# Causal attention and a gated expert: the scale of the gated values from the longest rows of v

## Chip, cores and metric

One core of a Trainium2 chip runs the whole program. The metric is device time in microseconds (us) of one execution; the kernel before took 555.05 us in the median of three runs (553.56 to 556.57).

## What is computed

The reference, cut to what matters. Batch 4, 12 heads, 448 positions, head size 64; weights come as 64-bit floats, the rest as 32-bit ones.

```python
scores = q @ k.T / 8, masked causally
attn = softmax(scores)
x = (attn @ v) laid out as [1792, 768]
a = x @ w1; b = x @ w2          # 768 x 1024 each
out = ((a * b) @ w3) @ w_out    # 1024 x 1024, 1024 x 768
```

## The kernel before, in words

All heavy products run on TensorE, most as sums of three half-precision products: a number is split into a scaled high part and a remainder. So each operand needs a scale (a power of two) that keeps it inside the range of 16-bit floats.

*Weights first.* The 64-bit words are decoded to fp32 on ScalarE (L727, L732), VectorE (L734, L737, L742) and GpSimd (L742). w3 and w_out are multiplied together once, in fp32: blocks of w3 are turned on TensorE (L824), copied out by ScalarE or VectorE (L830, L831) as `w3t`, and multiplied with `wof` (L836, 128 products). The result, and the 16 column blocks of w1 and w2 (`w16_0` to `w16_15`), get a scale from a sum of squares: ScalarE squares (L423), TensorE totals over partitions (L436, one column), VectorE makes the scale (L439, L442, L444); then a high part (`scaled`, L775 to L779) and a remainder (L459, L782) are made. A decoded block lives in one of four `da` tiles until its remainder is made.

*Attention.* The 48 heads go as 24 pairs, six per batch. A pair's scores (L612) are masked and their maxima taken on VectorE (L635), the exponentials on ScalarE (L639), the high part on any of three engines (L665, L667, L669), the remainder on VectorE (L672), both turned by DMA and multiplied with v (L692, L697). The result, x, is written as high and low part (L706, L709). `take_v` loads v for half a batch into `vr`, and ScalarE squares it (L423, sum into `vam`) to scale v; the squares themselves go to a `da` tile and are not used.

*Gating.* For each batch, `gate` multiplies x with w1 and w2 (L960 to L962), the two results are multiplied on VectorE, scaled by `y` and split, and `project` multiplies with the product of w3 and w_out (L1020 to L1022) and sends rows out. `norms` finds `y`: it multiplies x with itself on TensorE (L911, 24 products per batch: the largest squared length of a row of x is on the diagonal), takes the maximum (L914 to L917), combines it with the weights' scales and spreads the largest over partitions in `scales` (L407 to L418, one product with a diagonal, L410).

*Order.* Nothing runs in the order it is written. Each step is put into a list with a due time and a choice of engines, and a planner (`Program.order`) simulates all engines and writes out one instruction order for each. The numbers of `PLAN` set due times; an engine then runs its instructions strictly in that order. At the beginning TensorE has nothing to multiply, so `idle_work` gives it products of a tile of ones (L318), four at a time; the planner puts them wherever nothing else is ready.

```python
due += PLAN["wo1"]
take_wo(g, due + PLAN["wo"][g])
...
for _ in range(PLAN["nwarm"]):
    idle_work()
```

Of the kernel before, what the change touches and what calls it, by code (L numbers as in the profile page):

```python
# [26 lines left out]
PLAN = dict(nc=10, wstep=12.3531, soft=-605.1474, w0=476.7288, w34=1.8539, ab=3.6303, out=1.8146, gap=762.8813, lat=251.8676, begin=528.4141, wlead=403.7739, urgent=-286.1889, flex=536.535, sc=-408.2686, vo=420.0393, av=-116.9027, x=-168.3035, qlead=-2186.9998, rlead=-350.7116, v0=1307.3227, v1=8.0035, gram=2, nf=3, h0=-1, hv=0, ns=7, wo0=95.4929, wo1=14.6091, wom=-114.98, w3a=536.4028, w3l=90.5355, wd=-391.0133, wh=745.1126, wl=-928.1541, fin=-157.1358, ev=466.0051, po=[-164.0323, -537.4847, -467.5965, -398.0017, -379.2563, -815.7532, 309.0872, 47.1817, -120.6631, -601.6638, -125.3147, -350.4396, 41.4761, -121.6103, 339.5862, -519.8836, -967.096, -525.6425, 211.87, -136.3489, 191.5148, 668.7091, 243.9157, -640.695], wo=[-156.3639, 185.1511, 155.7329, -52.0715, 196.0473, -222.9949, 297.9082, 432.3035], w3=[15.1689, 214.9782, -115.2249, -1402.9929, -542.2877, 32.1711, -584.6361, 255.7376], tw=[-80.0272, -1064.4391, -227.6554, 134.6056, 384.2709, -735.5482, -250.8318, -265.1624, 67.0919, 261.8515, -168.3921, -339.4492, -398.6288, -878.4922, -309.2601, -175.1905], slack=0.62, pflex=-492.7855, fq=2, hlead=1597.3824, stick=248.1205, wfrom=6, join=0, quick=6, nwarm=34, w3h=[-97.0267, 4.4249, -687.8448, -92.0666, -119.591, 136.5231, 431.7171, 88.0246])  # L27
# [235 lines left out]
def tile_causal_attention_moe(ctx: ExitStack, tc: tile.TileContext, q, k, v, w1, w2, w3, wo, out):  # L263
# [156 lines left out]

    def squares(dst, src, junk, n, due, reads, writes):
# [64 lines left out]

    def take_v(b, half, due):
# [409 lines left out]
    def norms(b, due):  # L897
# [8 lines left out]
        def products():
            for c in range(4):
                n = min(P, S - c * P)
                for d in range(KD):
                    x = xb[:, d, 0, c * P : c * P + n]  # L910
                    nc.tensor.matmul(ps[:n, c * P : c * P + n], x, x, start=d == 0, stop=d == KD - 1)  # L911

        prog.add(due, (PE, 4 * KD * t_mm(P), products), [("xt", b % 2, d) for d in range(KD)], [key])
        prog.add(due, (DVE, t_dve(3 * P), lambda: nc.vector.tensor_reduce(out=t, in_=ps[:, : 3 * P], axis=AX.X, op=ALU.max)), [key], [tk])  # L914
        t2, t2k = small(1, "xnt2", 2)
        prog.add(due, (DVE, t_dve(D), lambda: nc.vector.tensor_reduce(out=t2[0:D], in_=ps[0:D, 3 * P : S], axis=AX.X, op=ALU.max)), [key], [t2k])
        prog.add(due, (DVE, 0.07, lambda: nc.vector.tensor_tensor(out=t[0:D], in0=t[0:D], in1=t2[0:D], op=ALU.max)), [tk, t2k], [tk])  # L917
# [10 lines left out]
        s, sk, e, ek = scales(am, ak, 1, "g", due)  # L928
# [192 lines left out]
```

## Time and profile before

| | |
|---|---|
| median of three runs | 555.05 us |
| profiled execution | 556.41 us, span 554.6 us |
| TensorE busy | 542.5 us, 98% |
| VectorE busy | 386.9 us, 70% |
| ScalarE busy | 319.6 us, 58% |
| GpSimd busy | 147.3 us, 27% |
| mean granted TensorE clock | 0.99 |

The span runs from the first to the last instruction; the execution's own time is 1.81 us longer. A product's end is modelled, so TensorE's busy time says little of its speed: the start of one product to the start of the next is its price. Engines appear as PE (TensorE), ACT (ScalarE), DVE (VectorE), POOL (GpSimd) and SP (the queue that issues DMAs).

### The profile page before, as it was taken

The page shows a single profiled execution, that of the slowest core. Times are in us where ns is not written, and L with a number is a line of the kernel's source. Part 1 is how long each engine was busy: PE and PEld are TensorE (multiplying, and loading weights), DVE is VectorE, ACT ScalarE, POOL GpSimd, SP SyncE. Part 2 cuts the span into 40 slices and gives each one's busy share as a digit, 9 for nine tenths or more (in the row PEclk, how much of TensorE's full clock was granted, in tenths as well). Part 3 has the DMA queues.
Part 4 walks back from the last instruction along what each step waited for, and adds up shares of the span by engine and source line. Part 5 has one row for each costly group of instructions (what it writes and reads, how often), then busy time and mean ns, then how long its engine had stood idle before and what let it go on. Part 6 is the DMA issues. An engine that isn't in the chain of part 4 may idle for free.

```text
span 554.6 us, 11026 instructions
## 1 busy us (share of the span) xinstructions
PE 542.5 (98%) x4008; PEld 314.0 (57%) x4008; DVE 386.9 (70%) x1062; ACT 319.6 (58%) x766; POOL 147.3 (27%) x113
## 2 busy tenths in 40 slices
PE   7899999998999999999999999999999999999996
PEld 7556556554655556655555556655555555555564
DVE  3564999897999999988773679879892883322100
ACT  3677897886798687776553478575461652111111
POOL 1010536554133224623222014422420322000000
PEclk9799999998999999999999999999999999999999
DMA  8999699997567366999746478987761664000011
GB/s 303 290 320 213 131 218 191 203 259 146 174 205 246 67 111 140 188 201 194 147 101 137 99 148 166 202 169 153 133 119 32 105 143 107 0 1 1 14 57 44
DMA packets 212663, 81.47 MB, mean 147 GB/s; under 512 B 193664, under 2 KB 209536, under 8 KB 212608
## 3 DMA queue, kind: packets, MB, share of 16 engines
q1 hardware_dynamic: 212608, 80.77, 65.7%
q8 instruction: 31, 0.51, 0.4%
q14 instruction: 24, 0.20, 0.1%
HBM read 43.78 MB, written 5.51 MB: 89 GB/s over the span
## 4 chain that ended last, share of the span: by engine, by line
PE 92%; DVE 2%; DMA 2%; ACT 1%; POOL 1%; issue 0%; SPq 0%; POOLq 0%; ACTq 0%; DVEq 0%
PE mm L836 10%; PE mm L960 9%; PE mm L962 9%; PE mm L961 9%; PE sc L612 7%; PE mm L1020 5%; PE mm L1022 5%; PE mm L1021 5%; PE tr L960 5%; PE tr L962 5%; PE tr L961 5%; PE av L697 4%; PE sc L836 3%; PE av L692 2%; DMA w34h<-in_moe_w_out_dram 2%; PE tr L612 2%
## 5 line engine op out<-in xcount | busy, mean ns | idle before, releaser
L960 PE MATMUL mm<-xt,w 128*128 128x448 f16 x252 | 88.9, 353 | 0.0
L962 PE MATMUL mm<-xt,w 128*128 128x448 f16 x252 | 88.9, 353 | 0.0
L961 PE MATMUL mm<-xt,w 128*128 128x448 f16 x252 | 88.8, 353 | 0.0
L639 ACT ACTIVATE p<-p,mx 128x384 f32<-128x384 f32 (+1 forms) x144 | 71.2, 496 | 28.9 <-DVE mx L635 28.8
L836 PE MATMUL mm<-wof,w3t 128*128 128x384 f32 x192 | 73.3, 521 | 2.0 <-ACT w3t L830 2.0
L672 DVE SCALAR_TENSOR_TENSOR ph<-p,rc,ph 128x384 f16<-128x384 f32 (+2 forms) x144 | 69.4, 539 | 1.9 <-POOL ph L669 1.8
L669 POOL TENSOR_SCALAR ph<-p,rc 128x128 f16<-128x128 f32 (+2 forms) x40 | 39.7, 1000 | 102.0 <-DVE rc L649 56.7
L960 PEld LDWEIGHTS <-w 128*128 128x128 f16 x384 | 37.5, 98 | 35.6 <-issue 1.8
L1020 PE MATMUL mm<-w34h,arena 128*128 128x384 f16 x176 | 57.6, 327 | 0.0
L1022 PE MATMUL mm<-w34h,arena 128*128 128x384 f16 x176 | 57.4, 326 | 0.0
L1021 PE MATMUL mm<-w34l,arena 128*128 128x384 f16 x176 | 57.4, 326 | 0.0
L962 PEld LDWEIGHTS <-w 128*128 128x128 f16 x384 | 37.5, 98 | 35.2
L961 PEld LDWEIGHTS <-w 128*128 128x128 f16 x384 | 37.5, 98 | 30.8
L836 PEld LDWEIGHTS mm<-wof,w3t 128*128 128x128 f32 x192 | 36.0, 200 | 28.3 <-issue 9.7
L960 PE MATMUL tr<-xt,w 128*128 128x448 f16 x132 | 46.6, 353 | 0.0
L961 PE MATMUL tr<-xt,w 128*128 128x448 f16 x132 | 46.5, 353 | 0.0
L962 PE MATMUL tr<-xt,w 128*128 128x448 f16 x132 | 46.5, 353 | 0.0
L612 PE MATMUL sc<-qkt 64*128 64x384 f16 (+6 forms) x416 | 42.9, 336 | 0.0
L453 POOL TENSOR_SCALAR v<-vr,v_s 128x512 f16<-128x512 f32 x17 | 31.3, 1840 | 41.2 <-PE av L697 32.9
L986 ACT CAST arena<-g 128x448 f16<-128x448 f32 x21 | 11.9, 565 | 48.9 <-DVE g L981 48.8
L981 DVE SCALAR_TENSOR_TENSOR g<-mm,y,at 128x448 f32<-128x448 f32 x16 | 10.9, 682 | 32.1 <-PE mm L962 32.0
L635 DVE CUSTOM_DVE_ANT_0 p<-sc,mask,qiv 128x384 f32<-128x384 f32 (+2 forms) x72 | 30.0, 479 | 4.1 <-PE sc L612 4.0
(189 smaller groups left out, 1037.3 us busy)
## 6 DMA issues: line engine op xcount, KB each, us to landing
arena<-in_moe_w_dram SPq DMA_DIRECT2D x11, 768.0 KB, 6.0
vr<-in_v_dram SPq DMA_DIRECT2D x24, 192.0 KB, 4.5
out_dram<-osb SPq DMA_DIRECT2D x24, 192.0 KB, 2.1
arena<-in_moe_w_dram SPq DMA_DIRECT2D x8, 512.0 KB, 7.4
xt<-in_moe_w_dram SPq DMA_DIRECT2D x5, 768.0 KB, 5.1
qkr<-in_k_dram SPq DMA_DIRECT2D x12, 224.0 KB, 4.3
qkr<-in_q_dram SPq DMA_DIRECT2D x12, 224.0 KB, 3.9
arena<-in_moe_w_out_dram SPq DMA_DIRECT2D x3, 768.0 KB, 7.9
```

Source lines behind the costliest of these rows:

```text
L453: (POOL, 1.17 * (t_pool(n) + 0.35e-3 * n + 0.16), lambda: nc.gpsimd.tensor_scalar(out=dst, in0=src, scalar1=s, scalar2=None, op0=ALU.mult)),
L612: nc.tensor.matmul(ps[rows if i == 2 else slice(0, P), at : at + w], qs[rows, c * P : c * P + n], ks[rows, 0:w], start=start, stop=stop)
L639: prog.add(due + 0.9, (ACT, t_act(w, pointers=1, acc=True), lambda o=o, u=u: nc.scalar.activation(out=o, in_=o, func=AF.Exp, scale=-1.0, b ...
L669: (POOL, 1.1 * (t_pool(w) + 0.35e-3 * w + 0.16), lambda src=src, r=r, h=h: nc.gpsimd.tensor_scalar(out=h, in0=src, scalar1=r, scalar2=None ...
L672: prog.add(due + 0.4, (DVE, t_dve(w) + 0.06, lambda src=src, r=r, h=h, l=l: nc.vector.scalar_tensor_tensor(out=l, in0=src, scalar=r, in1=h ...
L836: prog.add(due, (PE, 4 * t_mm(NH), lambda: nc.tensor.matmul(ps[:, :NH], w3t[slot(m)][:, g], wof[:, g, ns], start=g == 0, stop=g == KF - 1) ...
L960: nc.tensor.matmul(ps[:, :S], w[:, 0, d], xh, start=d == 0, stop=False)
L961: nc.tensor.matmul(ps[:, :S], w[:, 0, d], xl, start=False, stop=False)
L962: nc.tensor.matmul(ps[:, :S], w[:, 1, d], xh, start=False, stop=d == KD - 1)
L1020: nc.tensor.matmul(t, gh[:, fc, cs], w34h[:, fc, ns], start=fc == 0, stop=False)
L1021: nc.tensor.matmul(t, gh[:, fc, cs], w34l[:, fc, ns], start=False, stop=False)
L1022: nc.tensor.matmul(t, gl[:, fc, cs], w34h[:, fc, ns], start=False, stop=fc == KF - 1)
```

## The change

From batch 1 on, the bound on x's rows is taken from v: a row of x is an average of rows of v, so no head's part of it is longer than v's longest row in that head. `longest` sums the stored squares of v over the 64 elements of each row and head and takes the maximum over rows (two reductions on VectorE for each half of a batch); `bound` turns the 12 maxima per partition on TensorE, takes the maximum, adds up the heads with a product with ones, and multiplies with the scale of v twice. `norms` uses that instead of products of x with itself, and `power` stands for `scales` without spreading, since the bound is the same on all partitions. Batch 0 is left as it was. There are 50 quadruples of products on constants instead of 34. All numbers of `PLAN` that set due times are new, and one cost that the planner uses for loading halves of w3 (365 to 330 thousand bytes per us), so the order is another one throughout.

```diff
-PLAN = dict(nc=10, ..., gram=2, nf=3, ..., quick=6, nwarm=34, ...)
+PLAN = dict(nc=10, ..., gram=2, nf=3, ..., quick=6, nwarm=50, vb=1, ...)
...
+    def power(am, akey, name, due):
+        e, ek = small(1, f"{name}_e")
+        s, sk = small(1, f"{name}_s")
...
+        prog.add(due, (DVE, 0.09, lambda: nc.vector.reciprocal(out=s, in_=e)), [ek], [sk])
+        return s, sk, e, ek
...
+    def longest(b, half, sq, jk, due):
...
+            (g, c, lambda e=e: e.tensor_reduce(out=n, in_=sq.rearrange("p (n d) -> p n d", d=D), axis=AX.X, op=ALU.add))
+            for g, c, e in ((DVE, t_dve(4 * NP * D), nc.vector),)
+        ], [jk], [nk])
+        prog.add(due + 2, (DVE, 0.12, lambda: nc.vector.tensor_reduce(
+            out=m[:, half * NP : (half + 1) * NP], in_=n.rearrange("p (c h) -> p h c", h=NP), axis=AX.X, op=ALU.max)),
+            [nk], [mk + (half,)])
...
+    def bound(b, due):
...
+        prog.add(due + 3, (PE, 0.12, lambda: nc.tensor.transpose(ps[0:H, 0:P], m, ident)), [mk + (0,), mk + (1,)], [pk])
+        prog.add(due + 3, (DVE, t_dve(P), lambda: nc.vector.tensor_reduce(
+            out=top[0:H], in_=ps[0:H, 0:P], axis=AX.X, op=ALU.max)), [pk], [topk])
...
+        prog.add(due + 3, (PE, 0.03, lambda: nc.tensor.matmul(ps2[:, 0:1], ones[0:H], high, start=True, stop=True)), [topk], [pk2])
+        prog.add(due + 3, (DVE, 0.13, lambda: nc.vector.tensor_scalar(
+            out=t, in0=ps2[:, 0:1], scalar1=s, scalar2=s, op0=ALU.mult, op1=ALU.mult)), [pk2, sk], [tk])
...
+        if b >= PLAN["vb"]:
+            longest(b, half, j.bitcast(BF16), jk, due)
...
+        if half and b >= PLAN["vb"]:
+            bound(b, due)
...
-        ps, key = prog.lease("sc")
...
+        if b >= PLAN["vb"]:
+            t, tk = vt[b]
+        else:
+            t, tk = small(1, "xnt", 2)
+            ps, key = prog.lease("sc")
...
-        s, sk, e, ek = scales(am, ak, 1, "g", due)
+        s, sk, e, ek = power(am, ak, "g", due) if b >= PLAN["vb"] else scales(am, ak, 1, "g", due)
```

How the order moves, at three places. Lines of the changed kernel are 48 higher at the places shown (L727 is now L775) or 11 higher (L423 is now L434).

*ScalarE at the start, decoding the first blocks of w3 (512 columns) and w_out (768).* Before:

```order
L727 ACTIVATE da_108<-xt_101 128x768
L727 ACTIVATE da_107<-arena 128x512
L732 ACTIVATE w34l<-w34l 128x512
L727 ACTIVATE da_106<-arena 128x512
L830 COPY w3t_123<-tr_70 128x512
L727 ACTIVATE p_88<-w34h 128x768
L727 ACTIVATE da_106<-w34l 128x512
L830 COPY w3t_123<-tr_70 128x512
```

Now:

```order
L775 ACTIVATE da_107<-arena 128x512
L775 ACTIVATE da_108<-xt_101 128x768
L878 COPY w3t_123<-tr_70 128x512
L775 ACTIVATE da_106<-arena 128x512
L775 ACTIVATE p_88<-w34h 128x768
L775 ACTIVATE da_109<-w34h 128x512
L878 COPY w3t_123<-tr_70 128x512
```

The first half of w3's block is decoded first, and two decodes stand between its second half and the second copy of `w3t` as before, but the queue of transfers behind them is another: w3 half, w_out, w3 half, w_out, w3 half, instead of w_out, w3, w3, w3, w_out.

*ScalarE ahead of the last products of w3 and w_out: squares of weight blocks (into `wam`) and of v for batch 1 (into `vam`).* Before:

```order
L830 COPY w3t1_124<-tr0_70 128x512
L843 COPY xt512_101<-mm0_64 128x384
L423 ACTIVATE da2_108,vam1_140<-vr0_86 128x1536
L706 ACTIVATE xt448_100<-av0_63 128x448
L727 ACTIVATE da0_106<-arena_104 128x768
L732 ACTIVATE arena_104<-arena_104 128x768
L423 ACTIVATE w16_3_113,wam0_133<-da1_107 128x768
L732 ACTIVATE xt512_101<-xt512_101 128x768
L843 COPY xt512_101<-mm1_65 128x384
L450 ACTIVATE w34h_102<-xt512_101,w34_s2_132 128x768
L423 ACTIVATE w16_2_112,wam2_135<-da0_106 128x768
```

Now:

```order
L715 ACTIVATE pht0_94<-p32t0_91,rc1_152 128x448
L434 ACTIVATE w34h_102,w34m2_129<-xt512_101 128x768
L878 COPY w3t1_124<-tr0_70 128x512
L434 ACTIVATE w16_3_113,wam0_133<-da1_107 128x768
L775 ACTIVATE da0_106<-arena_104 128x768
L780 ACTIVATE arena_104<-arena_104 128x768
L754 ACTIVATE xt448_100<-av0_63 128x448
L891 COPY xt512_101<-mm1_65 128x384
L878 COPY w3t1_124<-tr0_70 128x512
L434 ACTIVATE da2_108,vam1_140<-vr0_86 128x1536
L823 ACTIVATE w16_1_111<-da3_109,w_s1_137 128x768
L434 ACTIVATE w16_2_112,wam2_135<-da0_106 128x768
```

The square of `w16_3` stood four places behind the square of v and now stands six ahead of it; the square of `w16_2` is now the first one behind it. The last step of pair 5's high part, `pht`, was GpSimd's and is now in this queue.

*VectorE at the same place: remainders of v and of weight blocks.* Before:

```order
L459 SCALAR_TENSOR_TENSOR v160_99<-vr1_87,v_s0_144,v160_99 128x512
L444 RECIPROCAL w34_s2_132<-inv_105 128x1
L742 ISA da0_106<-arena_104,da0_106 128x1536
L782 SCALAR_TENSOR_TENSOR w16_1_111<-da3_109,w_s1_137,w16_1_111 128x768
L439 TENSOR_SCALAR inv_105<-sc2_68 128x1
L459 SCALAR_TENSOR_TENSOR w34l_103<-xt512_101,w34_s2_132,w34h_102 128x768
L442 TENSOR_SCALAR inv_105<-inv_105 128x1
L444 RECIPROCAL w_s0_136<-inv_105 128x1
```

Now:

```order
L757 SCALAR_TENSOR_TENSOR xt448_100<-av0_63,xt448_100 128x448
L470 SCALAR_TENSOR_TENSOR v160_99<-vr1_87,v_s0_144,v160_99 128x512
L830 SCALAR_TENSOR_TENSOR w16_1_111<-da3_109,w_s1_137,w16_1_111 128x768
L507 TENSOR_REDUCE vsum0_155<-da2_108 128x24
L450 TENSOR_SCALAR inv_105<-sc2_68 128x1
L450 TENSOR_SCALAR inv_105<-sc3_69 128x1
L510 TENSOR_REDUCE vlong0_153<-vsum0_155 128x6
```

The first reduction of v's squares comes directly behind the remainder of `w16_1`, its maximum three places later. The decode addition that VectorE made here (L742) is gone from the place; GpSimd makes it.

## Rows read from the trace of the kernel before

**Rows 1.** Page, part 1: busy time of each engine, share, instructions.

```profile
PE 542.5 (98%) x4008; PEld 314.0 (57%) x4008; DVE 386.9 (70%) x1062; ACT 319.6 (58%) x766; POOL 147.3 (27%) x113
```

**Rows 2.** TensorE's waits: engine, line, releaser: us in total, times, longest.

```profile
PE sc L436 <- ACT w L423: 2.8, 2, 2.6
```

**Rows 3.** Stretches around the clock falls: busy us of each engine, PEclk, DMA, GB/s.

```profile
15.00:16.00 1.00, 0.47 (x1) 0.48 (x2) 0.99 (x3) 1.00 (x2) 0.00 (x0) 0.50 0.83 133
...
21.00:22.00 1.00, 1.00 (x9) 1.00 (x8) 0.10 (x1) 0.10 (x1) 0.00 (x0) 0.63 0.92 320
...
134.00:135.00 1.00, 1.00 (x4) 0.57 (x3) 1.00 (x2) 1.00 (x3) 0.54 (x1) 0.69 0.07 17
...
137.00:138.00 1.00, 1.00 (x3) 0.52 (x3) 0.00 (x0) 0.97 (x3) 0.00 (x0) 0.60 1.06 207
```

**Rows 4.** Stretches of 20 us, the same columns: 80 to 100 us.

```profile
80.00:100.00 20.00, 20.00 (x170) 12.49 (x167) 19.79 (x56) 16.53 (x48) 11.35 (x8) 1.00 1.00 209
```

**Rows 5.** Chain of waits, in order of time: start us, us, what.

```profile
104.86 0.44 PE tr L824 x4
...
133.55 0.16 PE sc L436
...
265.31 1.31 PE sc L911 x24
...
471.74 1.31 PE sc L911 x24
```

**Rows 6.** Timeline of TensorE, the start: start us, us, engine, line, operation, tiles [idle].

```profile
6.79 0.83 PE L318 MATMUL sc<-ones 128*128 128x128 bf16 x12
7.46 0.39 PE L318 MATMUL mm<-ones 128*128 128x128 bf16 x4
...
12.92 0.63 PE L824 MATMUL tr<-ident,arena 128*128 128x128 f32 x4 [1.48 <-DVE arena L737]
15.53 5.49 PE L836 MATMUL mm<-wof,w3t 128*128 128x384 f32 x8 [1.98 <-ACT w3t L830]
```

**Rows 7.** Timeline of ScalarE, the start, the same columns.

```profile
9.62 0.67 ACT L732 ACTIVATE w34l<-w34l 128x512 int32<-128x512 uint32 x1 [1.71 <-DMA w34l<-in_moe_w_dram]
10.93 0.66 ACT L727 ACTIVATE da<-arena 128x512 f32<-128x512 f32 x1 [0.63 <-DMA arena<-in_moe_w_dram]
...
13.54 0.89 ACT L727 ACTIVATE p<-w34h 128x768 f32<-128x768 f32 x1 [1.48 <-DMA w34h<-in_moe_w_out_dram]
...
14.88 0.59 ACT L830 COPY w3t<-tr 128x512 f32<-128x512 f32 x1
```

**Rows 8.** Timeline of ScalarE ahead of the wait at 133.55.

```profile
129.09 1.48 ACT L423 ACTIVATE da<-vr 128x1536 bf16<-128x1536 f32 x1 [4.53 <-POOL v L453]
...
132.57 0.84 ACT L423 ACTIVATE w<-da 128x768 bf16<-128x768 f32 x1
```

**Rows 9.** Timeline of VectorE, pair 5's first maximum to the remainder of w16_0.

```profile
111.53 0.60 DVE L635 CUSTOM_DVE_ANT_0 p<-sc,mask,minus 128x384 f32<-128x384 f32 x1
...
118.89 1.47 DVE L646 TENSOR_SCALAR rc<-sm 128x7 f32<-128x7 f32 x1
...
127.64 1.37 DVE L782 SCALAR_TENSOR_TENSOR w<-da,w_s,w 128x768 f16<-128x768 f32 x1
```

**Rows 10.** VectorE's two reductions of the products: ns min/median/max, first and last start.

```profile
L914 DVE TENSOR_REDUCE xnt<-sc x4: 547/556/559, 147.3 to 473.1; 128x1 f32<-128x384 f32 x4
...
L916 DVE TENSOR_REDUCE xnt<-sc x4: 205/206/206, 148.2 to 473.6; 64x1 f32<-64x64 f32 x4
```

**Rows 11.** Timeline of GpSimd at the same time.

```profile
118.47 1.86 POOL L742 TENSOR_TENSOR da<-da,xt 128x768 int32<-128x768 int32 x1 [3.82 <-ACT p L639]
```

**Rows 12.** Timeline of TensorE, the first products of batch 0's gating.

```profile
147.10 0.36 PE L960 MATMUL tr<-xt,w 128*128 128x448 f16 x1
147.30 0.35 PE L961 MATMUL tr<-xt,w 128*128 128x448 f16 x1
```

More of the change, by code (lines that the diff above doesn't have):

```diff
@@ L419, in scales @@
         return s, sk, e, ek
+    def power(am, akey, name, due):
+        e, ek = small(1, f"{name}_e")
+        s, sk = small(1, f"{name}_s")
+        prog.add(due, (DVE, 0.07, lambda: nc.vector.tensor_scalar(
+            out=e.bitcast(I32), in0=am.bitcast(I32), scalar1=0x7F800000, scalar2=None, op0=ALU.bitwise_and)), [akey], [ek])
+        prog.add(due, (DVE, 0.07, lambda: nc.vector.tensor_scalar(
+            out=e, in0=e, scalar1=LEAST, scalar2=2.0**-14, op0=ALU.max, op1=ALU.mult)), [ek], [ek])
+        prog.add(due, (DVE, 0.09, lambda: nc.vector.reciprocal(out=s, in_=e)), [ek], [sk])
+        return s, sk, e, ek
     def squares(dst, src, junk, n, due, reads, writes):
@@ L485, in tile_causal_attention_moe @@
     vam = {}
+    vlong, vt = {}, {}
+    def longest(b, half, sq, jk, due):
+        if half == 0:
+            vlong[b] = small(H, "vlong", 2)
+        m, mk = vlong[b]
+        n, nk = small(4 * NP, "vsum", 2)
+        prog.add(due + 2, [
+            (g, c, lambda e=e: e.tensor_reduce(out=n, in_=sq.rearrange("p (n d) -> p n d", d=D), axis=AX.X, op=ALU.add))
[5 more added lines that the diff above has]
+    def bound(b, due):
+        m, mk = vlong[b]
+        s, sk, _, _ = vsc[b]
+        t, tk = small(1, "vt", 3)
+        top, topk = small(1, "vtop", 2)
+        ps, pk = prog.lease("sc", "tr")
+        prog.add(due + 3, (PE, 0.12, lambda: nc.tensor.transpose(ps[0:H, 0:P], m, ident)), [mk + (0,), mk + (1,)], [pk])
+        prog.add(due + 3, (DVE, t_dve(P), lambda: nc.vector.tensor_reduce(
+            out=top[0:H], in_=ps[0:H, 0:P], axis=AX.X, op=ALU.max)), [pk], [topk])
+        ps2, pk2 = prog.lease("sc", "tr")
+        high = top.bitcast(BF16).rearrange("p (n t) -> p n t", t=2)[0:H, :, 1]
+        prog.add(due + 3, (PE, 0.03, lambda: nc.tensor.matmul(ps2[:, 0:1], ones[0:H], high, start=True, stop=True)), [topk], [pk2])
+        prog.add(due + 3, (DVE, 0.13, lambda: nc.vector.tensor_scalar(
+            out=t, in0=ps2[:, 0:1], scalar1=s, scalar2=s, op0=ALU.mult, op1=ALU.mult)), [pk2, sk], [tk])
+        vt[b] = t, tk
     def take_v(b, half, due):
@@ L752, in raw @@
         dma(view(t) if view else t.rearrange("p (n t) -> p n t", t=2), src, due, (), key, n * P * 8,
-            rate=288e3 if view else 393e3 if n == DM else 365e3, count=768 if view else P)
+            rate=288e3 if view else 393e3 if n == DM else 330e3, count=768 if view else P)
         return t.rearrange("p (n t) -> p n t", t=2), key
@@ L901, in norms @@
         _, _, vi, vik = vsc[b]
-        t, tk = small(1, "xnt", 2)
         y, yk = small(KF, "y", 2)
-        ps, key = prog.lease("sc")
[L906 to L917, printed above, removed]
+        if b >= PLAN["vb"]:
[3 more added lines that the diff above has]
+            ps, key = prog.lease("sc")
+            def products():
+                for c in range(4):
+                    n = min(P, S - c * P)
+                    for d in range(KD):
+                        x = xb[:, d, 0, c * P : c * P + n]
+                        nc.tensor.matmul(ps[:n, c * P : c * P + n], x, x, start=d == 0, stop=d == KD - 1)
+            prog.add(due, (PE, 4 * KD * t_mm(P), products), [("xt", b % 2, d) for d in range(KD)], [key])
+            prog.add(due, (DVE, t_dve(3 * P), lambda: nc.vector.tensor_reduce(out=t, in_=ps[:, : 3 * P], axis=AX.X, op=ALU.max)), [key], [tk])
+            t2, t2k = small(1, "xnt2", 2)
+            prog.add(due, (DVE, t_dve(D), lambda: nc.vector.tensor_reduce(out=t2[0:D], in_=ps[0:D, 3 * P : S], axis=AX.X, op=ALU.max)), [key], [t2k])
+            prog.add(due, (DVE, 0.07, lambda: nc.vector.tensor_tensor(out=t[0:D], in0=t[0:D], in1=t2[0:D], op=ALU.max)), [tk, t2k], [tk], port=True)
@@ L918, in norms @@
         am, ak = small(1, "gam", 2)
         ik = [("inv", w, fc) for w in range(3) for fc in range(KF)]
-        prog.add(due, (DVE, 0.08, lambda: nc.vector.tensor_tensor(out=y, in0=inv[:, 1], in1=inv[:, 2], op=ALU.mult)), ik, [yk])
+        prog.add(due, (DVE, 0.08, lambda: nc.vector.tensor_tensor(out=y, in0=inv[:, 1], in1=inv[:, 2], op=ALU.mult)), ik, [yk], port=True)
         prog.add(due, (DVE, 0.13, lambda: nc.vector.scalar_tensor_tensor(
-            out=y, in0=inv[:, 0], scalar=vi, in1=y, op0=ALU.mult, op1=ALU.mult)), ik + [vik, yk], [yk])
+            out=y, in0=inv[:, 0], scalar=vi, in1=y, op0=ALU.mult, op1=ALU.mult)), ik + [vik, yk], [yk], port=True)
```

2 lines of the change are left out of this document (1 added, 1 removed).

## The prediction

> **What bounds the kernel now.** The page comes first: TensorE is busy for 542.5 of 554.6 us [rows 1], so the time is its work plus the few places where it waits or runs slowly. The execution took 556.41 us, 1.81 us of it outside the span, and it lies 1.36 us above the median of 555.05; sums below are made against 556.41, and 1.36 comes off at the end. Next, TensorE's waits: the longest is 2.6 us of the 2.8 under line 436 [rows 2], and the two others that matter stand ahead of the first products of w3 and w_out, 1.48 us at 12.92 and 1.98 at 15.53 [rows 6]. Then the clock beside them: 0.50 of full speed after the start's waits, from 15 us to the second in which 0.63 is granted (21 to 22, so until about 21.6), and again 0.69 and later 0.60 after the wait that ends at 133.55 (0.69 and 0.60 put the fall at 134.4 and the rise at 137.8) [rows 3]. The engine had sat idle just before both falls. Half speed loses half of the busy time: (21.6 - 15.53) / 2 = 3.0 us at the start, (137.8 - 134.4) / 2 = 1.7 us later. Everything else on the chain is TensorE following itself.
>
> VectorE matters in one stretch: it is busy for 19.79 of the 20 us from 80 to 100 [rows 4], so there it paces the softmax, and what it finishes late reaches TensorE through ScalarE's queue at 133.55.
>
> **The products of x.** The chain shows the 24 products of batches 1, 2 and 3 as 1.31 us each, with TensorE waiting for nothing [rows 5]. The order of the changed kernel has 24 of these products where there were 96, so 3 x 1.31 = 3.93 us of bounding work goes. Three spreading products (128 columns) go as well; 12 products on constants of that size start in 0.67 us [rows 6], 0.056 each, so 0.17. Three transposes come, priced by four in 0.44 us, 0.11 each, 0.33 together [rows 5]. Three products of one column come: one standing alone takes 0.16 us [rows 5], behind others it may be hidden, so 0 to 0.48 for the three; I take 0.15, since they stand inside long runs. **Sum: -3.6 us** (-3.9 to -3.3).
>
> **The start.** Before, the second transpose of w3's first block starts at 12.92 and the first product at 15.53, released by ScalarE's second copy of `w3t` (14.88 to 15.47), which stood behind two decodes [rows 6, 7]. Now w3's two halves are the first and third transfer instead of the second and fourth. The third transfer landed by 9.62; the second half's chain took 12.92 - 10.93 = 2.0 us from ScalarE's decode to the transpose [rows 6, 7], so the transpose can start at about 11.6. The copy now stands behind the decode of the fifth transfer; the bytes up to it are the same 3,072 KB whose last decode started at 13.54. One decode of 512 columns (0.66) and one copy (0.59) put the first product at about 14.8, 0.7 earlier [rows 7]. Meanwhile 36 products on constants (36 x 0.056 = 2.0 us) fill 12.1 to 14.1, so the gap before the first product is some 0.7 us instead of 1.98, and I take it that the clock stays up: -3.0. But 32 of the 64 new products on constants come behind the first product: 32 x 0.056 = +1.8. **Sum: -0.7 - 3.0 + 1.8 = -1.9 us.** Ends: +1.1 if the clock falls all the same, -3.7 if TensorE would have waited for data while the 32 run.
>
> **The wait at 133.55.** It was for the square of `w16_3`, ScalarE's last piece before it (132.57). ScalarE had sat idle for 4.53 us until 129.09, in front of the square of v [rows 8]. That square writes into the tile `da2`, which VectorE's remainder of `w16_0` still read until 129.01 (127.64 + 1.37), behind six remainders of pair 5 [rows 9]; the releaser named is GpSimd, done at the same time. In the new order the square of `w16_3` stands ahead of v's, and the first one behind v's is `w16_2`. Its total is placed in front of the same TensorE work as the total of `w16_3` was (115 of 128 products of w3 and w_out precede either), so TensorE would come to it at 130.9 (133.55 - 2.6) less the start's 1.9: 129.0.
>
> When is it there? From VectorE's first maximum of pair 5 to the end of the `w16_0` remainder before: 111.53 to 129.01, 17.5 us [rows 9]. The new order has a remainder of w34 (about 1.0) and one scaling (about 0.6) more in that piece and drops some small pieces: I take 18.8. Pair 5's scores stand 1.4 us of work earlier on TensorE (counted in the order with the durations of their kinds) and the start gives 1.9, so the maximum moves from 111.5 to 108.2, if VectorE keeps that pace. The remainder ends at 127.0, then come the square of v (1.48), the scaling of `w16_1` (0.89, ScalarE's time for 768 columns) and the square of `w16_2` (0.83) [rows 7, 8]: 130.2. TensorE waits 1.2 us, less than the waits ahead of either fall of the clock. **Sum: -2.6 - 1.7 + 1.2 = -3.1 us**; ends: -4.3 (no wait) and 0 (as long as before, clock included).
>
> **The reductions of v.** Six sums over 1,536 bf16 elements are new on VectorE; nothing like them is in the trace. Of reductions there are 384 elements in 0.556 us and 64 in 0.206 [rows 10]: 1.09 ns an element, 206 + 1,472 x 1.09 = 1.81 us each. The other end is ScalarE's square over as many elements, 1.48 us [rows 8]. I take 1.81, the same engine and kind. The Trainium skill, VectorE: DVE Perf Modes, section Rules for kernel authors, speaks against this part of the change: a reduction on the hot path runs at the lowest rate whatever its type and should be restructured. By that rule bf16 gains nothing; the reductions in the rows are at 1.09 ns, which agrees as far as fp32 goes; no row shows bf16. For batches 2 and 3 they lie where VectorE has idle time, and nobody is near waiting. For batch 1, TensorE's transpose of the lengths stands within the first sums of batch 0's gating, behind the second reduction. TensorE: 130.2, then the 13.5 us that lay between the old total and the first gating product at 147.10 [rows 12], less the clock's 1.7, then 15 gating products that begin 0.2 apart [rows 12], 3.0: 145.0. VectorE: 127.0 and 17.9 us of rows up to it in the order: 144.9. I take **+0.5 us** of wait, between 0 (also by the lower price) and 2. What follows (a maximum, a product, a multiplication) has the rest of batch 0's gating to be done in.
>
> **Sum:** -3.6 - 1.9 - 3.1 + 0.5 = -8.1, so 548.3 us in this execution and **547.0 us** in the median (548.3 - 1.36 = 546.95).
>
> **Rivals.** *The wait stays.* VectorE is saturated where pair 1 to 5 are done [rows 4]; if it does not get ahead as TensorE does, the square of `w16_2` is as late as that of `w16_3` was, the wait is over 2 us and the clock falls again. Against it: what stood in front of v's square now precedes it. Then the -3.1 is lost: 550.1 us.
>
> *The start gains nothing.* The products on constants did not keep the clock before, because TensorE idled behind them; a gap over 1.5 us at 12 to 15 us, if a landing comes later, gives the half speed back: +3.0, 550.0 us. For it: landings set this piece, at 10.93 and 13.54 within 0.1 us of ScalarE's rows. Against it: the gap is filled up to 0.6 us.
>
> *Slower: GpSimd holds VectorE.* VectorE's scaling of seven sums took 1.47 us at 118.89, under GpSimd's decode addition that ran from 118.47 to 120.33 [rows 9, 11]. The new order has 8 of these additions of weights on GpSimd where there were 5, and by my count four instead of two ahead of the `w16_2` total. Were VectorE held for two of them (2 x 1.86) on top of the 1.3 us more of rows, of one reduction (1.8) and of a wait for its tile by the next decode (1 to 2), and if it sets the pace as before, the total comes at 133.55 + 3.7 + 1.3 + 1.8 + 1.5 = 141.9 (8.3 late), and the same again is lost where the next weights of batch 0's gating become due, about 3 us: 556.4 + 8.3 + 3.0 - 3.6 = 564.1, 562.7 in the median; with only the first place, 559.7. It decides from the point where the total comes later than 140 us (133.55 + 3.6 + 2.8). The Trainium skill, SBUF - State Buffer, section SBUF: two separate sides, says that VectorE and GpSimd take their common port one at a time, for a whole instruction. The one row here agrees. Against it: VectorE has three decode additions fewer itself, and pieces of pair 5 moved from GpSimd to ScalarE.
>
> That the products would not be left out is no rival: the order shows them gone.
>
> **Chances.** A difference under 0.5%, 2.8 us, is about what a measurement of this kernel cannot tell from none: faster means under 552.3 us, slower over 557.8. The forecast, with its ends between 543.5 and 549: 0.50. The wait stays: 0.20. The start gains nothing: 0.14. Both of these: 547.0 + 3.1 + 3.0 = 553.1, 0.09. GpSimd holds VectorE: 0.07. Faster: 0.50 + 0.20 + 0.14, plus a little of the case with both, less a part of the first two rivals that runs over, 0.83. Slower 0.07, no difference 0.10. The range of eight in ten runs from 543.5, all waits gone (547.0 - 1.2 - 0.5 - 1.8, the last the end of the start's term) to 552.0, short of the case with both.
>
> **What would show it.** The chain without products of x from batch 1 on; the first product of w3 and w_out near 14.8 at a clock of 1.00, and 1.00 up to 22 us; ScalarE's square of `w16_3` ahead of v's; a wait of TensorE near 129 us under 2 us with the clock at 1.00 behind it; a reduction of 1,536 elements at 1.8 us. I am wrong if TensorE waits over 2 us anywhere from 20 to 190 us, above all for wam totals, for the transposes of the lengths or for w_out's blocks, or if the clock of 15 to 21 us is 0.50 again.

## The result, and the profile after

The changed kernel takes **546.17 us** in the median of six runs (545.65 to 547.72), the kernel before 554.92 beside it: ratio 0.9845, 95% interval 0.982 to 0.9869. Measured a second time (first experiment below) the ratio was 0.9893 (0.9866 to 0.992), so the gain is 6 to 8.7 us. The prediction was 547.0 us, between 543.5 and 552.0. The profiled execution took 547.72 us, span 545.9. One execution of experiment 2, the profiled one, took 3159.9 us and is left out of its ratio.

The page's part 1 of the changed kernel, and its row of the granted clock over the span's 40 slices:

```profile
PE 537.8 (99%) x4003; PEld 311.9 (57%) x4003; DVE 395.0 (72%) x1065; ACT 320.3 (59%) x766; POOL 148.6 (27%) x113
...
PEclk9999999999999999999999999999999999999999
```

TensorE is at work for 99% of the span where it was 98 [rows 1], and no slice is below nine tenths of full speed. TensorE's waits (engine, line, releaser: us in total, times, longest):

```profile
PE sc L570 <- DMA qkr<-in_k_dram: 1.1, 1, 1.1
PE mm L318 <- DVE ones L312: 1.1, 1, 1.1
PE av L740 <- DMA ptt<-pht: 1.0, 1, 1.0
PE mm L884 <- ACT xt L891: 0.4, 1, 0.4
PE tr L872 <- ACT qkt L574: 0.3, 1, 0.3
```

The waits for `w3t` at 15.53 and for the total at 133.55 [rows 2, 6] are gone; one for k's transfer (at 18.43) and one for a turned tile of pair data (at 224.05) are new in this execution, 1 us each. The start on TensorE:

```profile
13.69 2.80 PE L884 MATMUL mm<-wof,w3t 128*128 128x384 f32 x8
16.32 0.60 PE L872 MATMUL tr<-ident,arena 128*128 128x128 f32 x4
...
18.43 0.60 PE L570 MATMUL sc<-ident,qkr 112*128 112x112 f32 x4 [1.06 <-DMA qkr<-in_k_dram]
19.60 0.63 PE L872 MATMUL tr<-ident,arena 128*128 128x128 f32 x4 [0.35 <-ACT qkt L574]
...
24.68 0.97 PE L660 MATMUL tr<-qkt 64*64 64x448 f32 x4
```

The first eight products take 2.63 us to the next start, at full speed, where they took 5.28 [rows 6]. ScalarE in front of the place of the old wait, and TensorE there:

```profile
121.28 0.84 ACT L434 ACTIVATE w<-da 128x768 bf16<-128x768 f32 x1
...
125.28 1.48 ACT L434 ACTIVATE da<-vr 128x1536 bf16<-128x1536 f32 x1
...
127.80 0.84 ACT L434 ACTIVATE w<-da 128x768 bf16<-128x768 f32 x1
```

```profile
129.01 0.17 PE L447 MATMUL sc<-wam,ones 128*128 128x1 bf16 x1
...
139.41 1.47 PE L962 MATMUL sc<-xt 128*128 128x128 f16 x24
...
140.88 0.35 PE L1011 MATMUL mm<-xt,w 128*128 128x448 f16 x1
...
143.18 0.27 PE L521 MATMUL sc<-ident,vlong 128*12 128x128 f32 x1
```

The square of `w16_3` now runs at 121.28, v's follows without idle time, that of `w16_2` is done at 128.6, and TensorE comes to its total at 129.01 and waits for nothing. The x24 group is the only product of x with itself that is left.

Where the 8.7 us of the two spans come from: 133.55 - 129.01 = 4.5 up to the total (2.6 of it the old wait, so 1.9 before it); 147.10 - 140.88 = 6.2 at the first gating product, so 1.7 more, the old fall of the clock behind the wait [rows 3, 12]; and 2.5 more to the end, the products of three batches (3.6 by the prediction) less the wait of 1.0 at 224.

### The profile page after: what moved, and what is told of

Its sections match the earlier page's. It is cut to its first block, busy times and chain, and to the rows that moved or that the text cites. A ratio compares the mean times of both kernels' runs of the same rounds, so it can differ in the third digit from the quotient of the medians.

```text
span 545.9 us, 11024 instructions
## 1 busy us (share of the span) xinstructions
PE 537.8 (99%) x4003; PEld 311.9 (57%) x4003; DVE 395.0 (72%) x1065; ACT 320.3 (59%) x766; POOL 148.6 (27%) x113
## 4 chain that ended last, share of the span: by engine, by line
PE 91%; DMA 4%; DVE 3%; ACT 1%; issue 1%; SPq 1%; DVEq 0%; ACTq 0%
PE mm L884 9%; PE mm L1011 9%; PE mm L1012 9%; PE mm L1013 9%; PE sc L660 7%; PE mm L1071 6%; PE mm L1073 5%; PE mm L1072 5%; PE tr L1011 4%; PE tr L1013 4%; PE tr L1012 4%; PE av L745 4%; PE sc L884 3%; DMA qkr<-in_k_dram 3%; PE av L740 2%; PE tr L660 2%
## 5 line engine op out<-in xcount | busy, mean ns | idle before, releaser
L1011 PE MATMUL mm<-xt,w 128*128 128x448 f16 x264 | 93.1, 352 | 0.0
L1012 PE MATMUL mm<-xt,w 128*128 128x448 f16 x264 | 93.0, 352 | 0.0
L1013 PE MATMUL mm<-xt,w 128*128 128x448 f16 x264 | 93.0, 352 | 0.0
L687 ACT ACTIVATE p<-p,mx 128x256 f32<-128x256 f32 (+1 forms) x144 | 71.2, 496 | 29.7 <-DVE mx L683 29.7
L884 PE MATMUL mm<-wof,w3t 128*128 128x384 f32 x192 | 68.9, 497 | 0.4 <-ACT xt L891 0.4
L717 POOL TENSOR_SCALAR ph<-p,rc 128x128 f16<-128x128 f32 (+2 forms) x37 | 34.3, 934 | 104.6 <-DVE rc L697 62.4
L1071 PE MATMUL mm<-w34h,arena 128*128 128x384 f16 x184 | 60.2, 327 | 0.0
L1073 PE MATMUL mm<-w34h,arena 128*128 128x384 f16 x184 | 60.0, 326 | 0.0
L1072 PE MATMUL mm<-w34l,arena 128*128 128x384 f16 x184 | 60.0, 326 | 0.0
L464 POOL TENSOR_SCALAR v<-vr,v_s 128x512 f16<-128x512 f32 x17 | 29.1, 1710 | 52.8 <-PE av L745 51.6
L1011 PE MATMUL tr<-xt,w 128*128 128x448 f16 x120 | 42.3, 353 | 0.0
L1013 PE MATMUL tr<-xt,w 128*128 128x448 f16 x120 | 42.3, 352 | 0.0
L1012 PE MATMUL tr<-xt,w 128*128 128x448 f16 x120 | 42.3, 352 | 0.0
L660 PE MATMUL sc<-qkt 64*128 64x256 f16 (+7 forms) x402 | 41.8, 338 | 0.0
L715 ACT ACTIVATE ph<-p,rc 128x384 f16<-128x384 f32 (+2 forms) x65 | 30.3, 522 | 10.3 <-ACT p32t L687 4.3
```

What stands on the lines that cost most here:

```text
L660: nc.tensor.matmul(ps[rows if i == 2 else slice(0, P), at : at + w], qs[rows, c * P : c * P + n], ks[rows, 0:w], start=start, stop=stop)
L687: prog.add(due + 0.9, (ACT, t_act(w, pointers=1, acc=True), lambda o=o, u=u: nc.scalar.activation(out=o, in_=o, func=AF.Exp, scale=-1.0, b ...
L715: (ACT, t_act(w, pointers=1), lambda src=src, r=r, h=h: nc.scalar.activation(out=h, in_=src, func=AF.Copy, scale=r)),
L717: (POOL, 1.1 * (t_pool(w) + 0.35e-3 * w + 0.16), lambda src=src, r=r, h=h: nc.gpsimd.tensor_scalar(out=h, in0=src, scalar1=r, scalar2=None ...
L884: prog.add(due, (PE, 4 * t_mm(NH), lambda: nc.tensor.matmul(ps[:, :NH], w3t[slot(m)][:, g], wof[:, g, ns], start=g == 0, stop=g == KF - 1) ...
L1011: nc.tensor.matmul(ps[:, :S], w[:, 0, d], xh, start=d == 0, stop=False)
```

## The experiments

Times are ratios to the kernel before, run beside each kernel; 0.001 is 0.55 us. Numbers in brackets further down, as (4), are those of the experiments.

**1. The changed kernel again**, without an edit.

> The changed kernel once more, as the measure for the three runs beside it, with the granted clock of every execution. Ratio 0.982 to 0.987. If the clock's fall at the start is gone for good, all executions show 0.998 or more and lie within 2 us of each other; if the start was only luckier in the profiled one, some show 0.993 to 0.997 as the kernel before does.

547.73 us, ratio 0.9893 (0.9866 to 0.992), above what was expected; mean clock 0.998 to 0.999 in all five, spans 544.4 to 547.1, while the kernel before showed 0.992 to 1.000. The fall at the start is gone. The transfers vary: in this execution ScalarE's decode of the fifth one starts at 12.95 and not at 11.52, TensorE waits 0.93 us ahead of the first product, at 14.13, and 1.15 for a later half of w3, and the wait for k is not met. By the first scores the two executions are level again (24.71 and 24.68), and they took 547.73 and 547.72 us, so this variation does not explain the times.

**2. Squares of v to a free tile** (kernel before):

```diff
-        if not b:
-            j = j.rearrange("p t s f -> p (t s f)")[:, : 4 * NP * D]
+        if not b: j = j.rearrange("p t s f -> p (t s f)")[:, : 4 * NP * D]
+        elif b == 1: j = w16[9].rearrange("p t c f -> p (t c f)")
```

> The kernel before, with one edit: for batch 1 the unused squares of v go to a tile nobody reads at that time instead of the decode tile that VectorE's remainder of w16_0 still reads. The order of instructions is the same. Theory of the prediction: ScalarE sat idle 4.5 us in front of v's square for that tile alone. The square then starts some 4 us earlier, the square of w16_3 is done in time, TensorE's wait of 2.6 us at 133.55 is gone or under 0.5, and so is the clock's fall behind it (1.7): 3 to 4.3 us less than before, ratio 0.992 to 0.995. Rival: the square waited for GpSimd, which the trace names (the scaling of v, done at the same time), or for another engine: no change, wait 2.6 at the same place, ratio 1.000. A middle case: the wait goes but comes back at the next total, where VectorE's pace sets the end: 0 to 1.5 us less.

551.40 us in the median of seven executions, ratio 0.9953 (0.9935 to 0.9971): 2.6 us less (1.6 to 3.6), somewhat under the theory's 3 to 4.3 and over the middle case. Squares that nobody reads afterwards made ScalarE wait for their tile. The trace is shown with the edit's other run, 4.

**3. Four of 24 products of x** (kernel before):

```diff
-                for d in range(KD):
+                for d in range(1 if b else KD):
...
-start=d == 0, stop=d == KD - 1)
+start=d == 0, stop=d == KD - 1 or b > 0)
```

> The kernel before, with 4 of the 24 products of x with itself left for each of batches 1 to 3 (one of six per column block; the scale of the gated values of those batches is then not the one that the reference's bound needs, since 20 of 24 products are left out). All else, the order too, is the same. Theory: these products bind at full price, 3 x 20 x 1.31 / 24 = 3.3 us less, ratio 0.994. Rival: something else on VectorE or in the transfers sets the pace where they stand and TensorE waits for it instead: under 1 us less, ratio over 0.998.

551.85 us, ratio 0.9962 (0.9947 to 0.9978): 2.1 us less (1.2 to 2.9). Its chain of waits (start us, us, what) has

```profile
143.35 1.33 PE sc L911 x24
262.83 0.31 PE sc L911 x4
366.60 0.31 PE sc L911 x4
```

so each group is 1.0 us shorter. From the second group's start to the third's it is 103.8 us; before it was 104.8 (265.31 to 370.08 in that chain). So the products bind, between these two groups in full. The executions give 2.1 us of the 3.0 that three groups come to in the trace: the theory's 3.3 is outside their interval, and so is the rival's "under 1 us".

**4. Both edits.**

> The kernel before with both edits of the two runs ahead: squares of v of batch 1 to a free tile, and 20 of 24 products of x left out for batches 1 to 3. If the terms are independent, the sum of the two: 3.3 + 3 to 4.3, so 6.3 to 7.6 us less, ratio 0.986 to 0.989, which would leave some 1 to 2.5 of the changed kernel's 8.7 us for the start. Rival: what one gives is lost in the wait of the other: as much as the larger alone, about 3.5 us, ratio 0.994.

547.78 us, ratio 0.9883 (0.9861 to 0.9905): 6.5 us less (5.3 to 7.7), more than the larger alone, and by the intervals not to be told from the 4.7 of the two added up. ScalarE at the place:

```profile
123.17 1.49 ACT L423 ACTIVATE w<-vr 128x1536 bf16<-128x1536 f32 x1
...
126.69 0.86 ACT L423 ACTIVATE w<-da 128x768 bf16<-128x768 f32 x1
```

The square starts at 123.17 without idle time, not at 129.09 after 4.53 [rows 8], though GpSimd, the named releaser, is as before. TensorE in experiment 3, which still has the wait; then the stretch from 132 to 134 us (busy us of each engine, PEclk, DMA, GB/s) there and here:

```profile
131.07 0.16 PE L436 MATMUL sc<-wam,ones 128*128 128x1 bf16 x1 [2.06 <-ACT w L423]
```

```profile
132.00:134.00 2.00, 2.00 (x5) 1.09 (x4) 2.00 (x4) 2.00 (x5) 0.05 (x1) 0.50 0.77 174
```

```profile
132.00:134.00 2.00, 2.00 (x9) 1.13 (x8) 1.97 (x6) 1.61 (x5) 0.00 (x0) 1.00 1.02 228
```

In this pair wait and fall go together (in 11 they do not). The products of x of batch 0 start at 143.35 in experiment 3 and at 140.17 here: 3.2 us.

**5. The new code with the old numbers** (due times, 34 quadruples, transfer rate).

> The changed code with the numbers of before: due times, 34 quadruples on constants and the transfer rate as before, the bound from v for batches 1 to 3. The planner makes an order of its own from them. Theory of the prediction: of its 8.1 us, 3.6 are the products and belong to the code, 4.5 (start 1.9, wait at 133.55 3.1, less 0.5) belong to the new numbers. So 3.6 us less at most, minus 0 to 2 for reductions that nobody made room for on VectorE, ratio 0.993 to 0.998, with the clock's fall at 15 to 21 us and a wait near 133 still there. Rival: the products' leaving alone lets the planner's order dissolve the waits too: ratio 0.985 to 0.988. Rival on the other side: the six sums on VectorE, put where it is full, cost more than the products gave: ratio over 1.000.

563.48 us, ratio **1.0159** (1.0132 to 1.0185): the rival on the other side. TensorE's waits:

```profile
PE av L740 <- DMA ptt<-pht: 4.1, 2, 3.3
PE sc L447 <- DVE mx L683: 3.6, 1, 3.6
PE mm L884 <- ACT w3t L878: 2.7, 1, 2.7
PE sc L447 <- ACT w L434: 2.0, 1, 2.0
```

The 3.3 and 3.6 stand at 218.41 and 225.94; VectorE's sums stand at 133 and 145, the next at 251 us. The clock at 15 to 16 us is 0.50 as before, and it falls twice more, to 0.50 at 60 to 62 and at 228 to 230 us, behind a wait of 1.75 at 57.94 and the one of 3.6. So the two largest waits are not beside the sums (the 2.0, at 134.76, is); what fits best is that the list of steps has changed and the old due times no longer fit it, but no run took the sums alone out.

**6. The new numbers with the old computation** (`vb=4`).

> The new numbers with the old computation: products of x with itself for all batches, no sums of v; the planner makes an order of its own from them. Theory of the prediction: the numbers carry the start and the wait at 133.55 and the code 3.6 us, so this kernel is 3.6 to 4 us slower than the changed one, ratio 0.992 to 0.995. Rival: due times fit only the list of steps that they were found for, as the run with the old numbers and the new code suggests, which was 1.6% slower: ratio over 1.000, with several waits of TensorE over 1 us.

549.79 us, ratio 0.9905 (0.9882 to 0.9928). TensorE waits for next to nothing:

```profile
PE mm L318 <- DVE ones L312: 1.0, 1, 1.0
PE mm L884 <- ACT xt L891: 0.4, 1, 0.4
```

Of the gain, some 5.3 us (4.0 to 6.5) are to be had by the order alone. What the new bound gives on top is 0.7 us by one ratio of the changed kernel (0.9893, whose interval overlaps) and 3.3 by the other (0.9845). So the rival falls, and the theory's 3.6 to 4 us is not shown; the ratio is better than its 0.992 to 0.995. The four cases:

| | old numbers | new numbers |
|---|---|---|
| products of x | 1 | 0.9905 |
| bound from v | 1.0159 | 0.9845, 0.9893 |

The changed code also marks three small VectorE steps (L968, L971, L973) for the planner as steps that GpSimd can hold up (`port=True`). The description of the change leaves this out; it is in the code of experiments 5 and 6 alike, so no run separates it.

**7. Sums of batch 1 twice** (changed kernel):

```diff
-            (g, c, lambda e=e: e.tensor_reduce(...))
+            (g, c, lambda e=e: [e.tensor_reduce(...) for _ in range(2 if b == 1 else 1)])
```

> The changed kernel with each of batch 1's two sums of v's squares made twice, 3.5 us more on VectorE between 129 and 142. Theory: VectorE is busy without a gap there and the lengths come 0.8 us before TensorE wants them, so TensorE now waits about 2.7 us for the transpose of the lengths (or for another piece of VectorE just there), and 1 to 2 us more if the clock falls: 2.7 to 4.5 us more than the changed kernel, ratio to before near 0.991. Rival: the reductions lie beside other work and have room: under 0.7 us more.

551.16 us, ratio 0.9953 (0.9937 to 0.9969), 3.4 us over the changed kernel beside it. TensorE's two new waits are one in front of a total of a block of w16 and one at the transpose of the lengths:

```profile
139.78 0.16 PE L447 MATMUL tr<-wam,ones 128*128 128x1 bf16 x1 [1.08 <-ACT w L434]
145.86 0.28 PE L521 MATMUL sc<-ident,vlong 128*12 128x128 f32 x1 [1.40 <-DVE vlong L510]
```

They are 2.5 us together, at 143.18 + 2.7 = 145.9, as expected; the clock stayed at 1.00. In the changed kernel VectorE is busy for 23.93 of 24 us there, and the lengths are ready 0.8 us ahead (142.16 + 0.18 against 143.18). The stretch, and VectorE's timeline:

```profile
122.00:146.00 24.00, 24.00 (x153) 14.22 (x153) 23.93 (x58) 21.50 (x37) 12.72 (x6) 1.00 0.90 205
```

```profile
139.90 1.74 DVE L507 TENSOR_REDUCE vsum<-da 128x24 f32<-128x1536 bf16 x1
...
142.16 0.18 DVE L510 TENSOR_REDUCE vlong<-vsum 128x6 f32<-128x24 f32 x1
```

**8. Without the cover ahead of the first product** (changed kernel):

```diff
-        def products():
-            for i in range(4):
+        def products(quads=PLAN.setdefault("quads", [])):
+            quads.append(1)
+            for i in range(0 if 28 <= len(quads) <= 42 else 4):
```

> The changed kernel without the 15 quadruples on constants between the first transpose of w3 and the first product; the order of all else is the same. TensorE is then idle for some 3 us before its first product, as the kernel before was for 2 to 3. Theory: these products keep the clock; without them some or all executions have half speed for up to 6 us behind the first product: 1 to 3 us more in the median than the changed kernel, mean clock 0.993 to 0.997. Rival: the clock stays up without them: within 0.5 us, mean clock 0.999.

546.38 us, ratio 0.9881 (0.9852 to 0.991), mean clock 0.995 or 0.996 in all five. Neither theory: the clock falls every time, and no loss is seen (547.73 for the changed kernel beside it). TensorE's timeline, and one stretch with the clock ahead of the last two numbers:

```profile
12.64 4.54 PE L884 MATMUL mm<-wof,w3t 128*128 128x384 f32 x8 [1.27 <-ACT w3t L878]
17.02 0.60 PE L872 MATMUL tr<-ident,arena 128*128 128x128 f32 x4
...
23.58 0.97 PE L660 MATMUL tr<-qkt 64*64 64x448 f32 x4
```

```profile
14.00:15.00 1.00, 1.00 (x3) 0.52 (x2) 0.26 (x1) 0.96 (x2) 0.00 (x0) 0.50 1.34 234
```

Half speed costs 4.38 - 2.63 = 1.75 us on the eight products, but they start 1.05 us earlier than behind the cover (12.64 against 13.69: the copy of `w3t` is done at 12.68 there too, and the products on constants last 1.0 us longer), so the next step is 0.7 us later, and there the waits of 1.06 and 0.35 for k are not met: the scores come at 23.58, 1.1 us earlier than with the cover.

**9. Without the fill behind the first product**: the same edit with `43 <= len(quads) <= 50`.

> The changed kernel without the 8 quadruples on constants behind the first product; the order of all else is the same. The prediction counted them as 1.8 us of bounding work. Theory now: 12 of the 32 products stand in front of waits for data, and the last 20 (1.1 us) in front of the first scores: 0 to 1.1 us less than the changed kernel. Rival: all 1.8 less. Rival on the other side: the wait for k then stands bare, the clock falls, 1 to 3 us more.

545.84 us, ratio 0.9864 (0.9838 to 0.9891), against 0.9893 of the changed kernel beside it; the intervals overlap. In the traces the scores come at 22.97 where they came at 24.68 (24.71 in experiment 1):

```profile
22.97 0.97 PE L660 MATMUL tr<-qkt 64*64 64x448 f32 x4 [0.88 <-DVE w3t L879]
```

and the products of x of batch 0 at 138.2 instead of 139.4. So 1.7 us at the place and 1.2 further on: in the trace the rival, nearly the 1.8 of the prediction; the executions alone do not show a cost. The clock stays up without these 32 products (0.999 or more).

**10. Without both**: `28 <= len(quads) <= 50`.

> The changed kernel without all 23 quadruples on constants from the first transpose of w3 on: the 15 ahead of the first product and the 8 behind it; the order of all else is the same. Each alone gave up the clock for some 3 us without a later end (the 15), or brought the products of w3 and w_out 1.7 us forward (the 8). Theory: what the fall costs was hidden in the waits that the 8 filled, so with both gone it shows: no better than without the 8 alone, 0.987 to 0.989 of before, clock 0.995. Rival: the two add up: the products of w3 and w_out come 2.8 us earlier and the ratio is 0.982 to 0.985.

546.96 us, ratio 0.9853 (0.9824 to 0.9882), clock 0.995 or 0.996. The scores come at 23.18 and the products of x of batch 0 at 138.1, as in 9: the fall is again hidden, in the wait of 0.95 for `w3t` in front of the scores. In the traces the two don't add up. By the runs, 8, 9 and 10 can't be told from the changed kernel.

**11. A cover in the kernel before**, 28 products on constants in front of its first product:

```diff
-lambda: nc.tensor.matmul(
+lambda: [nc.tensor.matmul(ps[:, :P], ones, ones, start=True, stop=True)
+         for _ in range(28 if (m, n, g) == (0, 0, 0) else 0)] and None or nc.tensor.matmul(
```

> The kernel before with 28 products on constants (1.6 us) directly in front of its first product of w3 and w_out, where TensorE waits 2 to 3 us for the second copy of w3t; the order of all else is the same. The prediction gave 3.0 of the start's gain to a clock that stays up. Theory now: the fall goes (granted clock 1.00 from 15 to 22 us), the first eight products take 2.6 to 2.8 us instead of 4.1 to 5.5, but the transfers behind them set the pace again as in the changed kernel without its cover: 0 to 1.5 us less than before, ratio 0.997 to 1.000. The prediction's own price: 3.0 us less, ratio 0.9945. Rival: the clock falls all the same, because what precedes it decides and 1.6 us are not enough: no gain, ratio 1.000.

553.46 us, ratio 0.9991 (0.9967 to 1.0016): nothing clear of noise, and not the 3.0. The trace, of an execution of 555.89 us, shows what became of it:

```profile
15.20 2.85 PE L836 MATMUL mm<-wof,w3t 128*128 128x384 f32 x8 [0.71 <-ACT w3t L830]
...
19.72 2.75 PE L836 MATMUL sc<-wof,w3t 128*128 128x384 f32 x8
...
48.64 0.60 PE L522 MATMUL sc<-ident,qkr 112*128 112x112 f32 x4 [0.59 <-DMA qkr<-in_k_dram]
...
52.18 0.60 PE L522 MATMUL tr<-ident,qkr 112*128 112x112 f32 x4 [0.99 <-DMA qkr<-in_q_dram]
...
57.78 0.41 PE L522 MATMUL sc<-ident,qkr 112*128 112x112 f32 x2 [1.75 <-DVE inv L439]
...
134.72 0.16 PE L436 MATMUL sc<-wam,ones 128*128 128x1 bf16 x1 [2.16 <-ACT w L423]
```

```profile
60.00:61.00 1.00, 1.00 (x3) 0.68 (x2) 1.00 (x3) 0.15 (x1) 1.00 (x1) 0.50 0.82 186
```

The clock stays at 1.00 at the start, and the second block of products begins at 19.72 and not at 23.04 (in the trace of before), 3.3 us ahead. Then TensorE waits for k, for q and for VectorE's reading of two totals (L439), which stands behind the decode of a weight block that is taken up at 55.45; at 57.78 TensorE is where the kernel before was at 57.37. The lead is used up by transfers, which are issued no earlier than before (that block's at 46.48, before at 45.76).

Behind this wait the clock falls after all, to 0.50 from 60 to 62 us, so in this execution the fall has moved and not gone. The total of the old wait comes at 134.72, and behind it, though TensorE waited 2.16 us there, the clock stays at 1.00; the first gating product is at 146.58 (before 147.10). Five of the twelve executions, this one among them, had a mean clock of 0.996 or 0.997 and took 555.28 to 556.55 us; the other seven, at 0.999 or 1.000, took 551.81 to 553.51, in the median 1.25 less than the kernel before. That the fall at 60 us parts the two groups fits, but only one of the executions has a trace.

**12. Batch 0 as well** (`vb=0`, no products of x at all).

> The changed kernel with the bound from v for batch 0 as well, so that no products of x with itself are left; the planner makes an order of its own. If the order held, 1.3 us less than the changed kernel. Theory: it doesn't hold; with two more sums of 1.74 us on VectorE and an order that was not looked for, waits come back: ratio 0.99 to 1.01. Rival: 0.982 to 0.985.

555.25 us, ratio 1.0007 (0.9991 to 1.0022), waits of TensorE of 2.5 us at 223.88, 1.7 at 176.88 (the lengths of a batch), with the clock at 0.50 from 178 to 180 behind it, and 1.2 at 231.89. As in 5, one more edit to the list of steps under due times that were not made for it costs more than the products give.

## Why the prediction was right, point by point

The forecast is 0.8 us from the median, and part of that is luck. Term by term the two spans give -2.5 for the products (with a new wait) where -3.6 stood, -1.9 for the start as predicted but from other parts, -4.3 for the wait where -3.1 stood, and 0 for the reductions where +0.5 stood.

*The products of x, -3.6.* Right in mechanism, a little large: 3 x 1.0 us left out gave 2.1 (1.2 to 2.9) in the runs and 1.0 between two groups in the trace (3); with the new numbers the code gives 0.7 to 3.3 (6). From the first gating product on the changed kernel gains 2.5, since a wait of 1.0 for a turned tile, which the prediction did not have, stands against the 3.6.

*The start, -1.9.* The sum is what the trace gives (4.5 - 2.6 = 1.9), its parts are not. The first product comes at 13.69, not 14.8: ScalarE's decode of the fifth transfer starts at 11.52, where the prediction took the landing of as many bytes before, 13.54.

```profile
11.52 0.69 ACT L775 ACTIVATE da<-w34h 128x512 f32<-128x512 f32 x1 [0.54 <-DMA w34h<-in_moe_w_dram]
12.11 0.57 ACT L878 COPY w3t<-tr 128x512 f32<-128x512 f32 x1
```

And not the copy sets it: that is done at 12.68, and the products on constants last until 13.69. So -1.8 where -0.7 stood. (The rise of the clock, read as 21.6, is 21.7 by its row, 0.1 us of no weight.) Of the clock's -3.0 the mechanism was right (the fall goes where the gap is filled: changed kernel and 11; it is there where the cover is taken out: 8 and 10). **The step that failed is that the 3.0 us were counted as bound work without naming what is late next.** In the order of before keeping the clock there gave 0.5 us (-0.9 to 1.8) and not 3.0 (11), and in the new one its loss is hidden too (8, 10). The sum holds because a second error stands against the first product's: the new waits for k (1.06) and `qkt` (0.35) were not foreseen, and -1.8 - 3.0 + 1.8 + 1.4 is -1.6, 0.3 from the trace. The +1.8 of the 32 later products on constants is 1.7 in the trace (9).

*The wait at 133.55, -3.1.* The mechanism was shown: the tile `da2` held the square of v back, not GpSimd (2, 4). The size in the two traces is -4.3, the upper end, since TensorE does not wait for `w16_2` at all; the runs of experiment 2, which takes this wait alone away, gave 2.6 (1.6 to 3.6), so that not all of it need reach the end. TensorE's arrival was predicted for 129.0 and is 129.01, by the luck of the start's term. What was mis-sized is VectorE's piece from pair 5's first maximum to the remainder of `w16_0`: 18.8 us predicted, 16.4 measured (108.83 to 125.25 instead of 108.2 to 127.0), so that the square is ready at 128.6, not 130.2.

*The reductions, +0.5.* One takes 1.742 us (1.81 predicted):

```profile
L507 DVE TENSOR_REDUCE vsum<-da x6: 1736/1742/1753, 129.2 to 368.3; 128x24 f32<-128x1536 bf16 x6
```

The 1,152 elements that it has over the 384 of rows 10 take 1.186 us more, 1.03 ns each, close to the 1.09 of the fp32 ones. The Trainium skill, VectorE: DVE Perf Modes, section The perf-mode tier table, lists `tensor_reduce` at the lowest rate in bf16 as in fp32. The trace agrees: the whole instruction is 4% under the price by fp32 rows. The wait was 0, with 0.8 us to spare, and 7 shows that there is little more room than that: 3.5 us more of sums cost 3.4.

*The rivals.* The wait did not stay, and the start's gap did not come back. Whether GpSimd holds VectorE is less clear. VectorE's timeline, then GpSimd's, each at two places:

```profile
126.30 2.02 DVE L470 SCALAR_TENSOR_TENSOR v<-vr,v_s,v 128x512 f16<-128x512 f32 x1
...
146.70 0.72 DVE L470 SCALAR_TENSOR_TENSOR v<-vr,v_s,v 128x512 f16<-128x512 f32 x1
```

```profile
125.92 1.84 POOL L790 TENSOR_TENSOR da<-da,arena 128x768 int32<-128x768 int32 x1 [1.52 <-ACT w3t L878]
...
144.96 2.21 POOL L827 TENSOR_SCALAR w<-da,w_s 128x768 f16<-128x768 f32 x1
```

The same remainder takes 2.02 us beside GpSimd's addition and 0.72 at 146.70, where GpSimd scales a tensor. So 1.3 us are lost at the first place, and TensorE waits for nothing there; that the addition is the cause is not shown by a run, and GpSimd's being at work is not enough for it. The slower side did not come. A slower kernel from the same code there is, by another mechanism: with due times that were not made for the list of steps it loses 1.6% (5).

## What to carry to other kernels

A stall's price counts only once the next late thing is named: here a stretch at half speed, 3 us by itself, gave nothing clear of noise when it was taken away, since transfers came behind it, and in the new order putting it back showed no loss. Look at what an instruction writes for nobody: one unused result in a tile still being read cost 2.6 us, and the releaser that the trace names was another engine, done at the same time. Where an order is made from due times, code and numbers are one change: the code alone was 1.6% slower, the numbers alone 1.0% faster.

## What the runs showed that was not expected

The same order at the start gave falls of the clock of different length: 0.50 until the second at 21 in the kernel before [rows 3], with an idle time of 1.98 us ahead of it, but only to 19 us in experiment 3, after 2.23 us of idle time (TensorE's timeline, then two stretches):

```profile
15.21 4.54 PE L836 MATMUL mm<-wof,w3t 128*128 128x384 f32 x8 [2.23 <-ACT w3t L830]
```

```profile
18.00:19.00 1.00, 1.00 (x3) 0.47 (x2) 0.79 (x2) 0.00 (x0) 0.00 (x0) 0.50 0.87 292
19.00:20.00 1.00, 1.00 (x7) 0.69 (x6) 0.00 (x0) 0.00 (x0) 0.00 (x0) 1.00 0.90 369
```

So the price of a fall read from one execution can be half as much again as that of another: the eight products took 5.28 us there, 2.65 over those at full speed, and 4.37 here, 1.7 over. Nor does the length of a wait tell whether a fall follows: in experiment 11 one came behind 1.75 us and none behind 2.16. What sets either was not settled.

Over many executions falls are not quite free. Of the 68 of the kernel before that were timed beside the experiments, the six at a mean clock of 0.999 or 1.000 lie on average 1.6 us below the median of their group, and the six at 0.990 or 0.991 lie 1.5 us above. Whether the falls or the waits ahead of them cost this, the times don't show.
